# Attention and balanced expert layer on one core: token scaling moved into the attention, search steps split with ScalarE, operands rearranged

## The chip, the cores and the metric

The kernel runs on one core of a Trainium2 chip. The metric is the device time of one execution in microseconds (us), taken as the median of several runs. A ratio is the mean time of one kernel's fast runs over that of the other's fast runs of the same rounds, so it is not quite the ratio of the medians quoted beside it; its bracket is a 95% interval. All runs compared here are in the fast state, except two single looks (e7 and e10) whose state a single run cannot tell, and one run of the kernel before in the first batch, which counted as slow and is left out of the ratios.

In the profile, PE is TensorE (PEld its weight loads), DVE is VectorE, ACT is ScalarE, POOL is GpSimd. L266 is line 266 of the kernel that is being profiled.

## The reference

Attention without a softmax, then a layer of eight experts to which the tokens are dealt greedily, 576 to each:

```python
kv  = einsum('bhsd,bhse->bhde', k, v)            # B,H,S,D = 8,8,576,64
out = einsum('bhsd,bhde->bhse', q, kv)
x   = out / sqrt(mean(out**2) + 1e-6) * g_norm   # -> 4608 tokens x 512
logits = x @ w_gate                              # 8 experts
# go through all (token, expert) by falling logit; take it if the token
# is free and the expert has fewer than 576
for e in range(8):
    mask = assigned == e
    out[mask] = relu(x[mask] @ w1[e]) @ w2[e]    # 512 -> 1024 -> 512
```

## The kernel before

The kernel has three stages: the attention, which writes tokens to DRAM; a first search for the threshold that fills one expert; and the eight experts, in which TensorE multiplies for expert t while the other engines search the threshold and the token list of expert t+1.

A search step compares each token's best logit, `mx`, with 32 candidate thresholds. This is one VectorE instruction of 128 x 1152 elements, and TensorE then counts its result:

```python
def compare(over, cand, c0=0, c1=GC):                        # L266
    nc.vector.tensor_tensor(over[:, c0:c1],
        mx[:, c0:c1]...to_broadcast([P, c1 - c0, NCAND]),
        cand[:, 1:NCAND + 1]...to_broadcast([P, c1 - c0, NCAND]), op=AL.is_ge)

def candidates(s, lo, cand):
    nc.vector.tensor_scalar(cand, in0=away[:, s], scalar1=lo, scalar2=None, op0=AL.add)
...
sm = small_ps["step"][:, turn_of[0] % 2]                     # PSUM
ends, cand_ps = sm[:, 0:2], sm[:, 2:]
for g in range(G):                                           # four of them, VectorE
    nc.vector.tensor_scalar(ends[g * QP:(g + 1) * QP], in0=kk, scalar1=width[0:QP, s:s + 1],
                            scalar2=lo_was[0:QP], op0=AL.mult, op1=AL.add)
lo = ends[:, 1:2]
if s + 1 < NSTEP:
    compare(over, candidates(s + 1, lo, cand_ps))
```

The candidates from the second search on are in PSUM (`held_ps`). So the compare has **one input in SBUF and one in PSUM**.

The tokens come with an unscaled attention output and a factor, and VectorE scales them just before TensorE transposes them (five operations `xs` to an expert).

The search is a Python generator. Its `yield 4.6` says how much of TensorE's work (in us) is to be put in the program between two counts; the first layer's work comes in pieces of 0.487.

## Time and profile before

| | before |
|---|---|
| time, median of 3 runs | 712.15 us (708.46 to 715.15) |
| span of the profiled run | 709.6 us |
| first expert starts | 180.34 us |
| experts 0 to 7 together | 518.98 us |
| of that, TensorE busy | 509.62 us, so 9.4 us idle |

The two last rows are from a table of windows by expert, whose sum row is this (window lengths, then busy time of each engine):

```profile
sum 518.98, PE 509.62 PEld 397.33 DVE 333.63 ACT 89.80 POOL 244.81; mean PE 63.70 PEld 49.67 DVE 41.70 ACT 11.23 POOL 30.60
```

Two groups of the page, with busy time, mean ns of one, and the idle time before them and what ended most of it:

```profile
L266 DVE TENSOR_TENSOR over<-mx,held_ps 128x1152 bf16<-128x1152 f32 x42 | 56.9, 1354 | 1.5
L478 PE MATMUL n_ps<-best,over 128*128 128x32 bf16 x441 | 19.3, 179 | 21.1 <-DVE over L266 19.2
```

The 42 compares take 1354 ns each. Most of the 19.2 us that TensorE waits for them are waits of the first search, where nothing else runs (one of them is the 4.71 us in front of the first count).

### The profile page before, as it was taken

How to read it: one execution, taken by the hardware profiler on the slowest of the kernel's cores; microseconds unless marked ns; L12 is line 12 of the kernel's file. 1: busy time of each engine (PE TensorE's matmuls, PEld its weight loads, DVE VectorE, ACT ScalarE, POOL GpSimd, SP SyncE). 2: the span in 40 equal slices, each digit the busy share in tenths (PEclk: the TensorE clock that was granted, in tenths of full speed). 3: DMA queues.
4: the chain of work that ended last, by engine and by line, in shares of the span. 5: the costliest groups of instructions: out<-in, count | busy, mean ns of one | idle time of the engine just before them, and what ended most of it. 6: DMA issues, size and time to landing. Idle time of an engine off the chain costs nothing.

```text
span 709.6 us, 13280 instructions
## 1 busy us (share of the span) xinstructions
PE 616.8 (87%) x5370; PEld 482.7 (68%) x5370; DVE 443.3 (62%) x1393; ACT 155.9 (22%) x315; POOL 263.8 (37%) x249
## 2 busy tenths in 40 slices
PE   3787788214999899989998999999899999999994
PEld 2566666212778677857885788678677867877782
DVE  4344656888687778888878779887887545020011
ACT  1454555300211121022102111121112022112100
POOL 0100011002342562438344632735263659226322
PEclk9988977555999999999999999999999999999998
DMA  8987889405303600531081053108013843001001
GB/s 283 316 278 237 278 297 351 177 0 184 129 1 103 251 26 1 205 137 38 6 306 67 1 180 132 68 1 312 28 41 127 293 165 106 0 30 38 0 1 67
DMA packets 41405, 93.41 MB, mean 132 GB/s; under 512 B 3456, under 2 KB 3456, under 8 KB 41344
## 3 DMA queue, kind: packets, MB, share of 16 engines
q1 hardware_dynamic: 34752, 72.49, 29.1%
q0 software_dynamic: 5888, 20.06, 8.1%
q8 instruction: 42, 0.69, 0.4%
q14 instruction: 19, 0.16, 0.1%
q10 hardware_dynamic: 704, 0.02, 0.1%
HBM read 72.50 MB, written 20.05 MB: 130 GB/s over the span
## 4 chain that ended last, share of the span: by engine, by line
PE 74%; DVE 13%; issue 6%; DMA 4%; ACT 1%; POOL 1%; POOLq 0%; ACTq 0%; DVEq 0%
PE h_ps L798 35%; PE y_ps L847 20%; PE o_ps L370 3%; PE qt_ps L301 3%; PE y_ps L858 3%; PE kv_ps L313 3%; PE t_ps L747 2%; DVE over L266 2%; DMA xg<-x_dram,ids 2%; PE n_ps L478 2%; DVE xs L733 1%; DMA gw<-in_moe_w_gate_dram 1%; PE warm_ps L625 1%; DVE need L484 1%; DVE held_ps L524 1%
## 5 line engine op out<-in xcount | busy, mean ns | idle before, releaser
L798 PE MATMUL h_ps<-xt,w_sb 128*128 128x288 f32 x1024 | 260.1, 410 | 0.8 <-ACT xt L750 0.8
L798 PEld LDWEIGHTS h_ps<-xt,w_sb 128*128 128x128 f32 x1024 | 190.6, 190 | 55.4 <-issue 5.7
L801 ACT ACTIVATE hid<-h_ps 128x288 f32<-128x288 f32 x128 | 52.6, 411 | 208.1 <-PE h_ps L798 208.1
L847 PE MATMUL y_ps<-tw,sh 128*128 128x256 f32 x384 | 86.5, 380 | 0.0
L847 PEld LDWEIGHTS y_ps<-tw,sh 128*128 128x128 f32 x384 | 72.0, 190 | 9.3
L789 POOL TENSOR_TENSOR sh<-hid 128x512 f32<-128x512 f32 x32 | 41.7, 1303 | 94.4 <-ACT hid L801 94.3
L673 POOL DMA_INDIRECT xg<-x_dram,ids x40 | 38.6, 964 | 82.8 <-DVE ids L668 35.8
L750 ACT ACTIVATE xt<-t_ps,g_col 128x512 f32<-128x512 f32 (+1 forms) x40 | 25.8, 645 | 161.6 <-PE t_ps L747 161.6
L847 PE MATMUL y_ps<-w_sb,hid 128*128 128x256 f32 x256 | 57.8, 381 | 0.0
L266 DVE TENSOR_TENSOR over<-mx,held_ps 128x1152 bf16<-128x1152 f32 x42 | 56.9, 1354 | 1.5
L818 DVE TENSOR_TENSOR y_sb<-y_ps,u 128x512 f32<-128x512 f32 x24 | 16.4, 684 | 63.8 <-PE y_ps L847 63.8
L756 POOL DMA_INDIRECT out_dram<-y_sb,outs x32 | 33.4, 1043 | 52.1 <-issue 36.7
L847 PEld LDWEIGHTS y_ps<-w_sb,hid 128*128 128x128 f32 x256 | 48.1, 190 | 6.6
L524 DVE TENSOR_SCALAR held_ps<-held_ps,width 32x2 f32<-32x2 f32 x144 | 41.3, 287 | 5.3
L779 POOL TENSOR_TENSOR tw<-w_sb 128x512 f32<-128x512 f32 x32 | 39.9, 1269 | 12.4 <-DMA w_sb<-in_moe_w_dram 12.3
L478 PEld LDWEIGHTS <-over 128*128 128x128 bf16 x441 | 17.5, 97 | 38.8 <-DVE over L266 27.5
L370 PE MATMUL o_ps<-kvx,qt 64*64 64x72 f32 x1152 | 32.9, 261 | 9.8 <-issue 9.2
L733 DVE TENSOR_TENSOR xs<-xg 128x512 f32<-128x512 f32 (+1 forms) x40 | 31.9, 809 | 14.7 <-DMA xg<-x_dram,ids 8.1
L478 PE MATMUL n_ps<-best,over 128*128 128x32 bf16 x441 | 19.3, 179 | 21.1 <-DVE over L266 19.2
L370 PEld LDWEIGHTS o_ps<-kvx,qt 64*64 64x64 f32 x1152 | 26.8, 160 | 15.5 <-issue 14.1
L378 DVE TENSOR_REDUCE ms<-sq 128x8 f32<-128x512 f32 x36 | 24.1, 681 | 20.1 <-ACT sq L376 19.9
L327 POOL COPY kvx<-kv 64x512 f32<-64x512 f32 x16 | 9.8, 609 | 71.3 <-DVE kv L321 70.9
(203 smaller groups left out, 831.9 us busy)
## 6 DMA issues: line engine op xcount, KB each, us to landing
w_sb<-in_moe_w_dram SPq DMA_DIRECT2D x16, 1024.0 KB, 6.3
w_sb<-in_moe_w_dram SPq DMA_DIRECT2D x8, 2048.0 KB, 13.3
k_sb<-in_k_dram SPq DMA_DIRECT2D x16, 576.0 KB, 5.4
v_sb<-in_v_dram SPq DMA_DIRECT2D x16, 576.0 KB, 5.8
q_sb<-in_q_dram SPq DMA_DIRECT2D x16, 576.0 KB, 5.6
x_dram<-o_sb SPq DMA_DIRECT2D x16, 576.0 KB, 4.3
x_dram<-o_sb SPq DMA_DIRECT2D x4, 288.0 KB, 4.2
xg<-x_dram,ids POOLq DMA_INDIRECT x40, 5.4
```

Source lines behind the costliest of these rows:

```text
L266: nc.vector.tensor_tensor(over[:, c0:c1], mx[:, c0:c1].rearrange("p (c o) -> p c o", o=1).to_broadcast([P, c1 - c0, NCAND]), cand[:, 1:NCA ...
L370: nc.tensor.matmul(o_ps[n * HP:(n + 1) * HP, rp, (2 * r2 + l) * W:(2 * r2 + l + 1) * W], lhsT=turned_q[bn][ks, block // 2, l * HP:(l + 1) ...
L478: nc.tensor.matmul(n_ps, lhsT=over[:, c:c + G].rearrange("p c n -> p (c n)"), rhs=best[:, :, c:c + G], start=(c == 0), stop=(c == GC - G))
L524: nc.vector.tensor_scalar(ends[g * QP:(g + 1) * QP], in0=kk, scalar1=width[0:QP, s:s + 1], scalar2=lo_was[0:QP], op0=AL.mult, op1=AL.add)
L673: tokens = nc.gpsimd.indirect_dma_start(out=xg[0:nr].rearrange("p h w -> p (h w)"), out_offset=None, in_=x_dram, in_offset=bass.IndirectOf ...
L733: nc.vector.tensor_tensor(xs[0:nr].rearrange("p (h d) -> p h d", h=H), xg[0:nr, :, 0:D], xg[0:nr, :, D:D + 1].to_broadcast([nr, H, D]), op ...
L756: put = nc.gpsimd.indirect_dma_start(out=out, out_offset=bass.IndirectOffsetOnAxis(ap=ids_of[t][0:nr, n:n + 1], axis=0), in_=y_sb[0:nr, :] ...
L779: in_order(nc.gpsimd.tensor_tensor(o[:, m:m + 2], x[:, m:m + 2], y[:, m:m + 2], op=AL.subtract))
L789: in_order(nc.gpsimd.tensor_tensor(o[:, ms], x[:, ms], y[:, ms], op=op))
L798: nc.tensor.matmul(h_ps, lhsT=w1[:, 2 * (d % 2) + d // 2, f * P:(f + 1) * P], rhs=xt[:, d, cs], start=(d == 0), stop=(d == DC - 1))
L801: nc.scalar.activation(hid[:, f, cs], h_ps, ACT.Relu)
L847: nc.tensor.matmul(p_ps[:, n], lhsT=left[:, f, n * P:(n + 1) * P], rhs=right[:, f], start=(f == 0), stop=(f == FH - 1))
```

## The change

Its intent: take the scaling, and the wait it makes, out of the experts; take work off VectorE by giving a step's ends and candidates to ScalarE; put search operands into PSUM, so that VectorE and GpSimd collide less (the trace of before shows one such collision: 1.34 us instead of 0.46); and order the first layer by halves of the tokens, so that fewer token blocks are needed before it can begin. The core of the diff:

```diff
-        nc.gpsimd.tensor_copy(o_sb[:, :, :, D:D + 1]..., inv)
+        for t in range(T):                     # in the attention
+            if c0 + T <= last_own:
+                nc.gpsimd.tensor_tensor(xo[:, t], o_sb[:, t, :, 0:D], inv[...].to_broadcast([P, H, D]), op=AL.mult)
+            else:
+                for h in range(H):
+                    late.append(lambda t=t, h=h: nc.scalar.mul(xo[:, t, h], o_sb[:, t, h, 0:D], inv[...]))
...
-    for nm, shape in (("step", (2, NCAND + 3)), ("cut", (2, GC)), ("mx", (GC,)), ...
+    for nm, shape in (("hi", (2,)), ("cut", (2, GC)), ("mx", (GC,)), ..., ("half", (NB,)), ("rise", (2, GC))):
...
+    KNOWN = 1.6
+    def candidates(s, lo):
+        cand = small("cand_a", NCAND + 1)                      # a tile in SBUF
+        nc.scalar.activation(cand, row_f[:, 0:NCAND + 1], ACT.Identity, scale=width[:, s:s + 1], bias=lo)
+        return cand
...
-            yield 4.6 if s > 0 else 0.4 if first else 2.0 if t == 1 else 4.0
+            yield (4.6 if t == 0 else 4.8 - KNOWN) if s > 0 else 0.4 if first else 2.0 if t == 1 else 2.4
...
+                yield KNOWN
-                lo_was, (ends, cand_ps) = lo, pieces()
+                lo_was, ends = lo, small("ends", 2)
                 for g in range(G):
-                    nc.vector.tensor_scalar(ends[g * QP:(g + 1) * QP], in0=kk, ...)
+                    nc.scalar.activation(ends[g * QP:(g + 1) * QP], kk, ACT.Identity, scale=..., bias=...)
-                    compare(over, candidates(s + 1, lo, cand_ps))
+                    compare(over, candidates(s + 1, lo))
...
-            nc.vector.tensor_tensor(xs[0:nr]..., xg[0:nr, :, 0:D], xg[0:nr, :, D:D + 1].to_broadcast(...), op=AL.mult)
...
-        for f, c in [(f, c) for f in units for c in range(2)] if t else [(f, c) for c in range(2) for f in units]:
+        for c, f in [(c, f) for c in range(2) for f in units]:
```

## The prediction

> **What bounds the kernel now.** I read the page first, then a table of windows by stage, then the chain of waits, then TensorE's own timeline. The page's busy lines say which engine fills the span, and its list of waits says who holds it up.
>
> ```profile
> span 709.6 us, 13280 instructions
> ...
> PE 616.8 (87%) x5370; PEld 482.7 (68%) x5370; DVE 443.3 (62%) x1393; ACT 155.9 (22%) x315; POOL 263.8 (37%) x249
> ...
> PE 74%; DVE 13%; issue 6%; DMA 4%; ACT 1%; POOL 1%; POOLq 0%; ACTq 0%; DVEq 0%
> ```
>
> TensorE (PE) carries 74% of the chain that ended last. The stages differ, so I cut the span at the starts of the eight experts (columns: window, length, busy time and instructions of each engine, granted clock, DMA share, GB/s):
>
> ```profile
> 30.00:137.00 107.00, 78.17 (x2208) 64.91 (x2200) 61.29 (x145) 55.96 (x110) 10.72 (x23) 0.79 0.81 282
> 137.00:180.30 43.30, 13.74 (x105) 7.73 (x105) 35.99 (x144) 2.06 (x3) 4.93 (x5) 0.56 0.26 85
> 180.30:250.35 70.05, 67.69 (x367) 52.12 (x367) 52.01 (x173) 12.12 (x25) 30.30 (x26) 0.98 0.35 124
> 250.35:316.94 66.59, 64.25 (x352) 50.09 (x351) 55.20 (x176) 11.55 (x24) 29.66 (x25) 1.00 0.27 94
> 316.94:382.50 65.56, 63.73 (x359) 50.37 (x359) 52.18 (x176) 11.55 (x24) 32.39 (x28) 1.00 0.28 103
> 450.00:514.70 64.70, 62.21 (x343) 48.52 (x343) 53.77 (x174) 10.98 (x23) 31.23 (x28) 1.00 0.29 104
> 514.70:578.70 64.00, 64.00 (x330) 49.61 (x326) 41.20 (x128) 11.56 (x24) 32.71 (x28) 1.00 0.40 145
> 578.70:640.30 61.60, 61.60 (x284) 48.49 (x284) 18.86 (x30) 11.56 (x24) 31.61 (x27) 1.00 0.23 75
> ```
>
> Three stages: attention to 137 us; a serial first search (VectorE busy 36 of 43 us) to 180 us; experts from 180 to 699 us. Expert 6 shows an expert with no search: 61.6 us, TensorE without a gap. The others take 63 to 70. TensorE's timeline shows what fills the difference:
>
> ```profile
> 239.31 0.66 PE L747 MATMUL t_ps<-ident,xs 128*128 128x128 f32 x4 [2.32 <-DVE xs L733]
> 305.85 0.66 PE L747 MATMUL t_ps<-ident,xs 128*128 128x128 f32 x4 [2.35 <-DVE xs L733]
> 377.39 0.63 PE L747 MATMUL t_ps<-ident,xs 128*128 128x128 f32 x4 [1.83 <-DVE xs L733]
> 509.51 0.63 PE L747 MATMUL t_ps<-ident,xs 128*128 128x128 f32 x4 [1.86 <-DVE xs L733]
> ```
>
> The bracket is TensorE's idle time and its releaser: the transposes of the next expert's tokens wait for VectorE to scale them. That is what the change takes away.
>
> How much is there? Per expert TensorE needs 128 first-layer records at 0.244 us (31.24 us for 128 in the chain), 112 second-layer ones at 0.216, 16 of the rest block at 0.234, about 2.1 us of transposes, and 0.23 us for each of 7 search counts. I laid this out in program order, with the kernel's own pacing numbers, and compared the experts' measured starts (180.34, 250.35, 316.94, 383.25, 448.01, 515.53, 578.61). The excess over uninterrupted work is 5.5, 3.1, 2.6, 1.3, 3.8 and 0.3 us for experts 0 to 5: 16.6 us, of which some 9.4 are visible idle gaps. This is the ceiling of what any repair of these waits can return.
>
> [...]
>
> ```profile
> 221.49 0.46 DVE L563 SCALAR_TENSOR_TENSOR here<-two,here 128x288 f32<-128x288 bf16 x1
> 287.32 1.34 DVE L563 SCALAR_TENSOR_TENSOR here<-two,here 128x288 f32<-128x288 bf16 x1
> 286.63 1.72 POOL L789 TENSOR_TENSOR sh<-hid 128x512 f32<-128x512 f32 x1
> ```
>
> The same operation takes 0.46 us alone and 1.34 beside GpSimd, whose own took 1.72 instead of 1.27.[...]
>
> **The change, part by part.**
>
> Token scaling. Five VectorE operations of 0.68 us or more leave each expert, 31.9 us in all. Their time is off the path; what counts is the wait in front of the transposes. At the first expert the gather of block 0 has landed by 174.40 and its scaling takes 0.69, so transposes and everything after start about 0.7 us sooner; a little more if the gather starts nearer its indices (170.38 now, indices written at about 169.3). I take -0.9.
>
> The scaling moves to GpSimd in attention: 31 tiles at about 1.27 us (the duration of its 128x512 two-input operations) = 39 us spread over 100 us in which GpSimd is busy about a tenth. Five tiles go to ScalarE as 40 operations[...], in the first search, where ScalarE is idle and the tokens are not needed until 170. Free. But GpSimd's share is not: after the fourth and sixth batch VectorE runs the early choice (84.67 to 87.43 and 111.95 to 113.99), with some five operations that have two SBUF inputs[...] some 0.9 us: up to 4.5 us each time. In the trace VectorE is continuously busy there and feeds TensorE. About half should be hidden by gaps TensorE has at just those points (2.78 us before 89.86, 2.15 before 116.47): +2 each time, +1 in the last batch, -1 for 11% less written. I take +3.5, the term I trust least.
>
> Fewer buffers in flight let three writes instead of one go before the last loads: 2 extra, about 1 MB at 280 GB/s = 3.4 us later. The last load is issued at 99.90 and lands near 105; its second half is used at 117.5. Hidden.
>
> Ends and candidates on ScalarE. A search step loses 4 x 0.287 + 0.259 = 1.41 us of VectorE and gains five pointer-bias activations[...], plus two crossings: no shorter. Counts to next counts is still about 5 us of latency. But the step is split into 1.6 and 3.2 of nominal TensorE time, and each part is rounded up to whole pieces of 0.487: 4 + 7 = 11 instead of 10. So a step takes 5.65 us where it took 5.16, +3 us in six steps, and the last step's pause adds 2 before the assignment. Shorter pauses after it give some back. In the program's order the tokens' list for expert 1 comes 4.3 us later than before (in the sixth of seven products instead of the fifth), for expert 2 about 0, for later experts early enough.
>
> Search operands in PSUM remove the 0.9 us collisions: VectorE only, off the path.
>
> First layer by halves. Only three of five blocks must be transposed before the next expert starts, the first of them some 1.3 us later. This makes room for the gather. For experts 2 to 4 the gap between list and first transpose is over 10 us, more than the 5.4 us (median) to landing plus 1.5 for indices: their waits vanish, 2.6 + 1.3 + 3.8 = -7.7, less 0.7 for small remainders: -7. For expert 1's tokens: list 4 to 5 us later, landing about 7 us after issue (231.41 to 238.39 now), first transpose about 1 us later: the wait grows to 5 or 6 us: +1.5. For expert 2's tokens: same place within 1 us: 0.
>
> ScalarE runs in order: a search step waiting for VectorE's count, or one beside a 0.69 us eviction, delays a Relu. Between Relus it idles 1.53 us and has two PSUM buffers, so mostly hidden: +1.
>
> Sum: -0.9 + 3.5 - 7 + 1.5 + 0 + 1 = -1.9 us. From the 709.6 of the profile and the median of 712.15, 710. Because the pauses look tuned on a chip, and my position counting may be pessimistic for expert 1, I lean 2 us lower: 708.
>
> **Rivals.** A: all token waits vanish and attention costs nothing: -16.6 - 1 - 1 = about 693. For it: VectorE falls from 80% to some 60% in the experts. Against it: the gather's own landing stands behind the scaling in experts 0 and 1. B: GpSimd collisions are not hidden and the late list costs more: attention +9, expert 0 +4, ScalarE stalls +3, against -8: about 720.[...] Against it: the split that sends the last five tiles to ScalarE shows the author knew of it. C: the pieces cancel completely, 712.
>
> **Range and chances.** Runs of the same kernel spread from 708.46 to 715.15. With the attention term uncertain by 4 and the expert term by 6, the range is 699 to 718. Over 2% faster means under 697.9, nearly the ceiling of A: 0.09. Slower than 726.4 needs more than B: 0.03.
>
> **What would show it.** No scaling before transposes; idle before the transposes of experts 1 and 2's tokens released by the gather DMA, about 5 and 2 us; none for later ones. Search counts 5.6 us apart. The first search starts later than 137 by 2 to 5 us, with early-choice operations around 1 us; if it stays at 137 the attention term is wrong. Relu gaps longer than 1.53 followed by TensorE idle would show ScalarE in the way. Wrong if expert 0 no longer waits, or if the time falls under 699.

## More of the kernel before

At the start of each expert, GpSimd makes weight differences `tw` for the second layer, eight instructions of 128 x 512 in a row:

```python
for o, x, y in ((t1, b12, b11), (t2, b22, t1), (t3, b22, b12), (t4, t2, b21)):
    for m in range(0, FH, 2):
        in_order(nc.gpsimd.tensor_tensor(o[:, m:m + 2], x[:, m:m + 2], y[:, m:m + 2], op=AL.subtract))
```

The name `"mx"` in the PSUM list is a working copy that both kernels have; the `mx` that the compare reads is another tile, in SBUF in both.

## The result, and the profile after

The changed kernel takes **765.86 us** (764.18 to 766.57, four runs), the kernel before 712.02 in the same rounds: ratio 1.0754 [1.0701, 1.0808]. It is 7.5% slower, and the prediction (708, range 699 to 718) was wrong. The page's lines that answer to those in the prediction:

```profile
span 762.4 us, 13333 instructions
...
PE 633.4 (83%) x5370; PEld 489.3 (64%) x5370; DVE 397.6 (52%) x1158; ACT 241.2 (32%) x560; POOL 298.1 (39%) x271
...
PE 66%; DVE 19%; issue 6%; ACT 5%; DMA 3%; POOL 1%; POOLq 0%; ACTq 0%; DVEq 0%
```

VectorE did get less to do (397.6 us busy instead of 443.3), yet its share of the chain that ended last grew from 13% to 19%. So somewhere it has become the one that TensorE waits for. The windows by expert (columns as in the prediction) say where:

```profile
332.73:407.79 75.06, 66.43 (x361) 50.97 (x360) 50.06 (x134) 25.99 (x64) 32.10 (x27) 0.95 0.24 88
407.79:483.51 75.72, 67.13 (x358) 51.29 (x353) 50.18 (x138) 26.12 (x63) 32.84 (x29) 0.93 0.25 91
630.38:692.38 62.00, 62.00 (x285) 48.49 (x284) 9.05 (x25) 11.54 (x24) 30.69 (x27) 1.00 0.22 73
sum 570.91, PE 525.17 PEld 403.26 DVE 284.90 ACT 165.04 POOL 248.76; mean PE 65.65 PEld 50.41 DVE 35.61 ACT 20.63 POOL 31.10
```

The experts with a search take some 75 us instead of 65 to 67; expert 6 (from 630.38), which has none, takes 62.0 as before. The eight together grew by 570.91 - 518.98 = 51.9 us, nearly the whole of the 52.8 us by which the span grew; the first expert starts only 1.2 us later (181.56). TensorE's idle time in them went from 9.4 to 570.91 - 525.17 = 45.7 us, which is +36.4, and its busy time by +15.5 us for the same work. The granted clock (third column from the end: the share of full speed that TensorE's throttle let through) is 0.93 to 0.96 in experts 0 to 5, where it was 1.00 (0.98 in expert 0).

The groups of the page name the cause of the idle time:

```profile
L266 DVE TENSOR_TENSOR over<-mx,cand_a 128x1152 bf16<-128x1152 f32 x36 | 91.9, 2554 | 78.1 <-ACT cand_a L488 75.3
L508 PE MATMUL given_ps<-best,over 128*128 128x32 bf16 x441 | 19.6, 180 | 56.5 <-DVE over L266 54.8
L555 ACT ACTIVATE ends<-kk,ends,width 32x2 f32<-32x2 f32 x144 | 55.4, 385 | 33.5 <-DVE kk L550 30.3
```

The compare of the same size takes 2554 ns in the mean where it took 1354, and TensorE's wait for it has grown from 19.2 to 54.8 us, by 35.6, nearly all of the 36.4 us of new idle time. The row shows what is different: it reads `mx` and `cand_a`, both in SBUF. TensorE's timeline shows the waits one by one (start, length, instructions, and in brackets the idle time and its releaser):

```profile
246.74 1.12 PE L790 MATMUL t_ps<-ident,xg 128*128 128x128 f32 x4 [6.33 <-DMA xg<-x_dram,ids]
272.22 0.42 PE L508 MATMUL given_ps<-best,over 128*128 128x32 bf16 x9 [5.68 <-DVE over L266]
322.70 0.66 PE L790 MATMUL t_ps<-ident,xg 128*128 128x128 f32 x4 [2.58 <-DMA xg<-x_dram,ids]
346.43 0.42 PE L508 MATMUL given_ps<-best,over 128*128 128x32 bf16 x9 [8.63 <-DVE over L266]
346.69 4.93 PE L839 MATMUL h_ps<-xt,w_sb 128*128 128x288 f32 x14
```

Two more such waits are 8.59 us (before 422.40) and 6.38 us (before 497.22), and one of 5.95 lies before 572.3: one count wait in each of experts 1 to 5, 35.2 us together. The wait of 6.33 us is that for expert 1's tokens. What VectorE and GpSimd did in front of the count at 272.22:

```profile
263.77 8.39 DVE L266 TENSOR_TENSOR over<-mx,cand_a 128x1152 bf16<-128x1152 f32 x1 [2.13 <-ACT cand_a L488]
...
260.21 0.91 POOL L797 DMA_INDIRECT out_dram<-y_rest,outs  x1 [5.23 <-DVE y_rest L907]
261.13 2.51 POOL L820 TENSOR_TENSOR tw<-w_sb 128x512 f32<-128x512 f32 x2
263.58 2.50 POOL L820 TENSOR_TENSOR tw<-w_sb,tw 128x512 f32<-128x512 f32 x2
266.03 2.48 POOL L820 TENSOR_TENSOR tw<-w_sb 128x512 f32<-128x512 f32 x2
268.47 2.47 POOL L820 TENSOR_TENSOR tw<-tw,w_sb 128x512 f32<-128x512 f32 x2
```

The compare was released at 263.77, just after the third instruction of GpSimd's run of eight had begun at 263.58. It ended at 272.16: GpSimd's run ends at 268.47 + 2.47 = 270.94, and 1.2 us later, about the compare's own length, it is done. It was kept out by **all six instructions that were left**, the running one included, and not by that one alone. ScalarE then stood too (8.90 us before its next Relu), since it waited for TensorE.

### The profile page after: what moved, and what is told of

Its sections match the earlier page's. It is cut to its first block, busy times and chain, and to the rows that moved or that the text cites. A ratio compares the mean times of both kernels' runs of the same rounds, so it can differ in the third digit from the quotient of the medians.

```text
span 762.4 us, 13333 instructions
## 1 busy us (share of the span) xinstructions
PE 633.4 (83%) x5370; PEld 489.3 (64%) x5370; DVE 397.6 (52%) x1158; ACT 241.2 (32%) x560; POOL 298.1 (39%) x271
## 4 chain that ended last, share of the span: by engine, by line
PE 66%; DVE 19%; issue 6%; ACT 5%; DMA 3%; POOL 1%; POOLq 0%; ACTq 0%; DVEq 0%
PE h_ps L839 27%; PE y_ps L888 21%; DVE over L266 8%; PE y_ps L899 3%; PE qt_ps L301 3%; PE o_ps L372 3%; PE t_ps L790 2%; PE kv_ps L313 2%; ACT ends L555 2%; PE given_ps L508 2%; DMA xg<-x_dram,ids 2%; DMA gw<-in_moe_w_gate_dram 1%; DVE ms L380 1%; DVE need L514 1%; PE warm_ps L662 1%
## 5 line engine op out<-in xcount | busy, mean ns | idle before, releaser
L839 PE MATMUL h_ps<-xt,w_sb 128*128 128x288 f32 x1024 | 274.2, 423 | 0.8 <-ACT xt L793 0.8
L839 PEld LDWEIGHTS h_ps<-xt,w_sb 128*128 128x128 f32 x1024 | 195.9, 196 | 58.5 <-issue 4.1
L266 DVE TENSOR_TENSOR over<-mx,cand_a 128x1152 bf16<-128x1152 f32 x36 | 91.9, 2554 | 78.1 <-ACT cand_a L488 75.3
L830 POOL TENSOR_TENSOR sh<-hid 128x512 f32<-128x512 f32 x32 | 43.9, 1372 | 157.7 <-ACT hid L842 157.7
L714 POOL DMA_INDIRECT xg<-x_dram,ids x40 | 41.8, 1044 | 76.6 <-DVE held_ps L630 42.7
L508 PE MATMUL given_ps<-best,over 128*128 128x32 bf16 x441 | 19.6, 180 | 56.5 <-DVE over L266 54.8
L555 ACT ACTIVATE ends<-kk,ends,width 32x2 f32<-32x2 f32 x144 | 55.4, 385 | 33.5 <-DVE kk L550 30.3
L797 POOL DMA_INDIRECT out_dram<-y_sb,outs x32 | 31.4, 981 | 42.2 <-issue 28.6
L399 POOL TENSOR_TENSOR xo<-o_sb,inv 128x512 f32<-128x512 f32 x31 | 32.5, 1079 | 33.9 <-ACT sq L378 21.6
L820 POOL TENSOR_TENSOR tw<-w_sb 128x512 f32<-128x512 f32 x32 | 39.9, 1268 | 12.2 <-DMA w_sb<-in_moe_w_dram 12.0
L313 PE MATMUL kv_ps<-v_sb,k_sb 64*64 64x64 f32 x1152 | 28.2, 243 | 9.1 <-issue 9.1
L301 PE MATMUL qt_ps<-ident,q_sb 128*128 128x128 f32 x144 | 31.5, 348 | 4.3 <-ACT kvt L334 1.9
```

Of the source, the lines that this page charges most:

```text
L266: nc.vector.tensor_tensor(over[:, c0:c1], mx[:, c0:c1].rearrange("p (c o) -> p c o", o=1).to_broadcast([P, c1 - c0, NCAND]), cand[:, 1:NCA ...
L301: nc.tensor.transpose(t_ps[:, x, :], q_sb[:, (4 * n + x) * P:(4 * n + x + 1) * P], ident)
L313: nc.tensor.matmul(kv_ps[cs, l, r * D:(r + 1) * D], lhsT=k_sb[ls, r, j, :], rhs=v_sb[ls, r, j, :], start=(j < 2), stop=(j >= R - 2))
L508: nc.tensor.matmul(n_ps, lhsT=over[:, c:c + G].rearrange("p c n -> p (c n)"), rhs=best[:, :, c:c + G], start=(c == 0), stop=(c == GC - G))
L555: nc.scalar.activation(ends[g * QP:(g + 1) * QP], kk, ACT.Identity, scale=width[0:QP, s:s + 1], bias=lo_was[0:QP])
L714: tokens = nc.gpsimd.indirect_dma_start(out=xg[0:nr], out_offset=None, in_=x_dram, in_offset=bass.IndirectOffsetOnAxis(ap=ids[0:nr, n:n + ...
```

## The experiments

Ten kernels ran, all with correct results (the record has no e6 and no e9). A theory T and rivals were set against each other:

- **T**: the compare lost its PSUM input (the candidates went from PSUM to an SBUF tile, since ScalarE makes them) and, with both inputs in SBUF, is kept out by GpSimd's run (8.39 us instead of 1.36 at 263.77).
- **R1**: the two crossings to ScalarE, and ScalarE's work in the step, are what delays the counts.
- **R2**: the attention's scaling, or the halves of the first layer, cost it.

### e1: the changed kernel, with the compare's other operand in PSUM

The candidates stay where the change has them; a second copy of `mx` goes to PSUM, and the compare reads that.

```diff
+    now = {"mx": mx}
             nc.vector.tensor_tensor(mx, m, gone, op=AL.add)
+            now["mx"] = small_ps["mx_all"]
+            nc.vector.tensor_tensor(now["mx"], m, gone, op=AL.add)
-            over[:, c0:c1], mx[:, c0:c1]...
+            over[:, c0:c1], now["mx"][:, c0:c1]...
-                      ("rise", (2, GC))):
+                      ("rise", (2, GC)), ("mx_all", (GC,))):
```

> The changed kernel with one extra 36-element VectorE operation per search that keeps a second copy of the tokens' best values in PSUM; the compare of searches 1 to 6 reads that copy, so it has one SBUF input (the candidates of ScalarE) instead of two. Theory T (the compare lost 8 to 11 us in each of five experts because both its inputs are now in SBUF[...]): every compare returns to 1.36 us, no wait of TensorE for it over 1 us in the experts, time about 718 us (765.9 less 38 of waits and 10 of stretched first-layer matmuls). Rival S (ScalarE in order: ends and candidates there make the step longer and hold up Relus): stays above 750 us. Rival H (halves of the first layer): stays above 750 us.

Measured: **716.29 us** (715.01 to 719.66), ratio to the kernel before 1.005 [0.9983, 1.0116]. 50 us came back with one operand moved. The compare's row, the same compare in the same place, and the GpSimd pair that runs across it:

```profile
L269 DVE TENSOR_TENSOR over<-held_ps,cand_a 128x1152 bf16<-128x1152 f32 x36 | 48.9, 1357 | 73.4 <-ACT cand_a L491 70.6 <-ACT ends L558 2.8
...
265.09 1.36 DVE L269 TENSOR_TENSOR over<-held_ps,cand_a 128x1152 bf16<-128x1152 f32 x1 [2.13 <-ACT cand_a L491]
264.91 2.50 POOL L823 TENSOR_TENSOR tw<-w_sb,tw 128x512 f32<-128x512 f32 x2
```

1.36 us in the middle of GpSimd's run, where it had been 8.39, and neither engine slows the other. TensorE's waits for the counts in experts 1 to 5 are gone; what stays is one wait of 6.30 us for expert 1's tokens and one of 2.53 for expert 2's. R1 and R2 cannot be the bulk: ScalarE's part, the scaling and the halves are all still in.

### e2: the kernel before, with only the candidates moved to SBUF

The converse. VectorE still makes them (by another operation, a `tensor_tensor` instead of a `tensor_scalar`), so ScalarE has no part in it.

```diff
+    def in_sbuf(s, lo):
+        cand = small("cand_s", NCAND + 1)
+        nc.vector.tensor_tensor(cand, away[:, s], lo.to_broadcast([P, NCAND + 1]), op=AL.add)
+        return cand
-                    compare(over, candidates(s + 1, lo, cand_ps))
+                    compare(over, in_sbuf(s + 1, lo))
```

> The kernel before, whose only edit is that the candidates of a step from the second search on are written to SBUF instead of PSUM, still by VectorE. Theory T: in five of six searches a compare meets GpSimd's run of eight operations and lasts 8 to 11 us, so 30 to 45 us slower than before, about 745 to 757 us. Rivals S and H: no change, 712 us.

Measured: **761.0 us** (760.39 to 765.16), ratio 1.0697 [1.062, 1.0775]. That is somewhat more than expected, and it makes nearly all of the change's loss with none of the change's other parts.

```profile
L266 DVE TENSOR_TENSOR over<-mx,cand_s 128x1152 bf16<-128x1152 f32 x36 | 93.0, 2583 | 1.2
```

### e3: the changed kernel, with ends and candidates back on VectorE, in PSUM

```diff
-    def candidates(s, lo):
-        cand = small("cand_a", NCAND + 1)
-        nc.scalar.activation(cand, row_f[:, 0:NCAND + 1], ACT.Identity, scale=width[:, s:s + 1], bias=lo)
+    def candidates(s, lo, cand):
+        nc.vector.tensor_scalar(cand, in0=away[:, s], scalar1=lo, scalar2=None, op0=AL.add)
...
-                    nc.scalar.activation(ends[g * QP:(g + 1) * QP], kk, ACT.Identity, ...)
+                    nc.vector.tensor_scalar(ends[g * QP:(g + 1) * QP], in0=kk, ...)
```

> The changed kernel with ends and candidates back on VectorE and in PSUM; places of the search pieces, halves and token scaling stay as changed. Theory T: compares of 1.36 us, time 710 to 718 us, within 3 us of the run with the second copy in PSUM. Rival S: also near 712, but then the run with the copy in PSUM stays above 750. Rival H: above 750.

Measured: **714.2 us** (711.39 to 718.62), ratio 1.0013 [0.9943, 1.0083]. Beside e1 it says that, with the change's own pacing and every compare short again (1354 ns in the mean), it makes little who computes the ends: the medians differ by 2 us, the eight experts in the profiles by 1 (523.3 against 524.2), and the intervals overlap. Its expert 1 still waits 6.40 us for its tokens.

### e4: the kernel before, with only the scaling moved to the attention

> The kernel before with the token scaling alone moved into attention (GpSimd 31 tiles, ScalarE 5), everything else as before. Attention ends 2 to 3 us later, the first expert starts 1 us earlier after that, and the transposes wait for the gather alone: -1 for expert 1, up to -2 each for experts 2, 3 and 5. Sum about 707 us; 712 if the gather lands no sooner than VectorE was done; above 720 only if the scaling part is what made the changed kernel slow.

```diff
-        nc.gpsimd.tensor_copy(o_sb[...], inv)
+        ... xo = o_sb * inv on GpSimd, the last tiles on ScalarE, as in the change
-            nc.vector.tensor_tensor(xs[0:nr]..., xg..., op=AL.mult)
-            scaled.append(xs)
+            scaled.append(xg)
```

Measured: **701.72 us** (698.01 to 705.16), ratio 0.9838 [0.9758, 0.9918]. It beats both kernels, and by more than expected (the interval lies below 1, but on both sides of a gain of 2%). In its profile the waits before the transposes are 1.86 us (expert 1) and 0.71 us (expert 2), where they were 2.32 and 2.35, and none is over 0.3 us in the later ones.

### e5: e4, and the first layer by halves

```diff
-        for f, c in [(f, c) for f in units for c in range(2)] if t else [...]:
+        for c, f in [(c, f) for c in range(2) for f in units]:
```

(and the main loop's places for the transposes as in the change; the search's pauses stay those of before)

> The kernel with the scaling alone in attention (701.7 us) plus the first layer by halves and the later transposes of the change; places of the search pieces, VectorE's ends and candidates stay those of before. If the late list of the changed places is what the changed kernel still loses once its compare is mended (experts 0 and 1 took 73.8 and 69.7 us against 68.1 and 64.9): expert 0 about 67, expert 1 about 64.5, the waits of 1.86 and 0.71 us for the gather gone, 0.4 to 1 us more in each later expert, time 699 to 704 us. If the halves are what it loses: experts 0 and 1 above 70 and 67, time above 708.

Measured: **703.75 us** (699.8 to 706.07), ratio 0.990 [0.9862, 0.9938]. In the profiles, experts 0 and 1 take 66.3 and 64.4 us against 68.1 and 64.9 in e4, and each later one up to 1 us more: about nothing in sum. The halves did make room for the gather (one wait of 1.20 us is left in all), but in e4 there was little left to hide.

### e7 and e10: what keeps the compare out for a whole run?

Both keep two SBUF inputs. e7 makes GpSimd start its run of eight only after the fifth Relu, so that it no longer follows directly on the indirect DMA that GpSimd issues. e10 leaves it where it is and makes it 16 instructions of 256 elements.

```diff
-            for m in range(0, FH, 2):                                   # e10
-                in_order(nc.gpsimd.tensor_tensor(o[:, m:m + 2], ...))
+            for m in range(FH):
+                in_order(nc.gpsimd.tensor_tensor(o[:, m:m + 1], ...))

+            tc.add_manual_dep(made[0].ins, relu.ins.name, ...)          # e7: the run's first waits for a Relu
```

> The changed kernel with GpSimd's run of eight weight differences held until the fifth Relu of the first layer, so that GpSimd is idle for some us between its last indirect DMA issue and the run, as it was in expert 0, where a compare got in after one operation (2.2 us). If the run keeps VectorE out to its end only because it follows an indirect DMA issue directly: all compares under 2.7 us, time under 730. If the run's own operations keep it out: some compares still of 6 to 11 us in experts 1 to 5, time 750 to 770.

> The changed kernel with the run of eight GpSimd differences cut into sixteen of half the size, the same work. If a compare waits for one operation of the run: the long compares shrink from 8 to 11 us to under 3, time about 720. If it waits for the end of the run: they stay 8 to 12 us, as the run grows a little with its fixed costs, time 765 to 775.

Measured, one run each: e7 **720.94 us**, e10 **713.11 us**. In both no compare takes over 2.45 us (means 1502 and 1508 ns). A compare of e7 with the GpSimd pair that began during it, and one of e10 likewise:

```profile
278.25 1.63 DVE L266 TENSOR_TENSOR over<-mx,cand_a 128x1152 bf16<-128x1152 f32 x1 [2.38 <-ACT cand_a L488]
278.62 3.60 POOL L822 TENSOR_TENSOR tw<-tw,w_sb 128x512 f32<-128x512 f32 x2
```

```profile
258.61 1.45 DVE L266 TENSOR_TENSOR over<-mx,cand_a 128x1152 bf16<-128x1152 f32 x1 [2.13 <-ACT cand_a L488]
258.70 3.99 POOL L820 TENSOR_TENSOR tw<-w_sb,tw 128x256 f32<-128x256 f32 x4
```

Four instructions of 256 elements take 2.77 us together in e10 (at 262.66), two of 512 in the changed kernel 2.48 (at 266.03).

In e7 VectorE waits 0.27 us for the rest of the GpSimd instruction that ran when it came, and then GpSimd gives way: its next pair takes 3.60 us instead of 2.5. So in e7 the two take turns, one instruction at a time. In the changed kernel and in e2 they did not: all ten compares that met the run in experts 1 to 5 waited until its end (6.7 to 9.7 us over their 1.36; the longest took 11.05 us, in e2), at whatever point of an instruction they came, from just before its start to 1.15 us into it. In expert 0, where GpSimd had idled for 12 us before the run, they got in after one instruction in both kernels (2.20 and 1.71 us). So in these kernels the long exclusion took both, the run directly behind an indirect DMA's issue and instructions of 512 elements; each was taken away in one run. Both together are not always enough: at 537.55 in the changed kernel a compare met another run of 512-element instructions (`sh`) behind an indirect DMA, and got in after one (1.93 us). There GpSimd had stood for 0.08 us between the first two, while those of the long cases follow without a pause. **Why** a run keeps its hold, the profile does not show, and this stays open.

### e8: e4, with GpSimd's scaling held until after VectorE's early choice

```diff
+        made = compare(over0, cand0, c0, c1)          # the last operation of the early choice
+        for do in held_back:
+            tc.add_manual_dep(do().ins, made.ins.name, ...)
...
-                nc.gpsimd.tensor_tensor(xo[:, t], ...)
+                held_back.append(lambda t=t: nc.gpsimd.tensor_tensor(xo[:, t], ...))
```

> The kernel with the scaling alone in attention, with GpSimd's scalings of the fourth and sixth batch held until VectorE's early choice there is done. If the choice's two-input operations beside GpSimd are what made attention end 2.5 to 4 us later: the first expert's start 2 to 4 us earlier and about 699 us. If not, 701.7 as before; if GpSimd's copies of the next batch then come late, 703 to 706.

Measured: **698.73 us** (694.58 to 703.6), ratio 0.9826 [0.9783, 0.987], the lowest median of all that ran. The two early choices take VectorE 2.75 and 2.04 us, where e4's take 4.93 and 4.51, and the first count of the first search is at 135.51 us, where e4 has it at 140.94. The ratios do not tell e8 from e4, e5 or e12; the early choices do. A middle expert of it, with no gap and the clock at full:

```profile
374.20:438.20 64.00, 64.00 (x353) 50.14 (x351) 50.12 (x166) 11.56 (x24) 30.43 (x28) 1.00 0.30 106
```

### e11: e1, and the pauses of the kernel before

After e1, the eight experts still take 524.2 us where e5's take 510.1. What e5 lacks is ScalarE's part, the change's other pauses, and its rearranged small operands and deferred operations. Are these 14 us the late list of tokens?

```diff
-    KNOWN = 1.6
+    KNOWN = 1.4
-            yield (4.6 if t == 0 else 4.8 - KNOWN) if s > 0 ...
+            yield (4.6 if t == 0 else 4.6 - KNOWN) if s > 0 ...
-        yield 5.0 if t == 1 else 5.4
+        yield 5.4 if t == 0 else 3.6 if t == 1 else 4.0
```

> The changed kernel with a copy of mx in PSUM (as in e1) and, beside that, the old pacing of a search: 3 + 7 pieces of TensorE's work to a step instead of 4 + 7, and the pause that a search leaves behind taken off the pause before the assignment. Theory ([...]what is left of the loss against the better kernels is the late list of tokens): the steps come 5.2 us apart instead of 5.7, the list for expert 1 some 4 us sooner, the 6.3 us wait before expert 1's transposes falls to 1 to 3 us, the 2.5 us one of expert 2 to 0 to 1; time 706 to 710, ratio 0.990 to 0.997. Rival (ScalarE's place in a step makes it longer than 5.2 us, and its 2 crossings cannot be hidden in 10 pieces): TensorE waits at the counts, 0.3 to 1 us each, and the time stays at 713 to 718.

Measured: **710.75 us** (708.68 to 718.25), ratio 1.0003 [0.9947, 1.0059]: in between. The counts that make expert 1's list came at 232.81 us instead of 237.82 (1.7 of the 5.0 us are an earlier start of the first expert), and the 6.30 us wait for expert 1's tokens shrank to 0.2; the eight experts take 518.1 us instead of e1's 524.2. But the steps did not come 5.2 us apart. They stayed at 5.7 on average (counts at 190.52, 196.27, 202.19, 207.65). In part this is because TensorE now waits for a Relu that stands behind a step in ScalarE's order; two steps of this search have such a wait, of 0.49 us each:

```profile
200.63 1.72 PE L842 MATMUL h_ps<-xt,w_sb 128*128 128x288 f32 x6 [0.49 <-ACT hid L845]
```

So the rival was right about the steps and the theory about the list. Some 6 us of the 14 went with the late list. Some 8 us stay against e5's experts (518.1 against 510.1). 3.7 of them are visible as waits, for Relus, counts and sums (5.0 us idle in experts 0 to 5 instead of 1.25); the other 4 lie in time that counts as busy, and no run here takes them apart. The Relu waits belong to the ScalarE step; that the rest of the 8 us does too is not shown, since e5 lacks other edits as well and e3 with the old pauses did not run.

### e12: e8 and the halves together

The edits of e5 and e8 in one kernel.

> Both best parts together: scaling in the attention with GpSimd's share held until after VectorE's early choice (as in e8), and the first layer by halves with the old pauses (as in e5). If halves are worth what e5 and e4 showed (experts 0 and 1 some 2.3 us shorter together, the six later ones 0.3 us longer each on average), they cancel: 698 to 700, ratio 0.981 to 0.986. If e5's first two experts keep their gain and the later ones' loss was chance: 696, ratio 0.979.

Measured: **700.33 us** (697.44 to 705.29), ratio 0.9858 [0.9804, 0.9912]. As the first of the two expectations had it, the halves bring nothing on top of e8.

### The versions side by side

| kernel | compare's inputs | scaling | halves | ends made by | median us | ratio |
|---|---|---|---|---|---|---|
| before | SBUF, PSUM | in the experts | no | VectorE | 712.02 | 1 |
| after | SBUF, SBUF | attention | yes | ScalarE | 765.86 | 1.0754 |
| e2 | SBUF, SBUF | in the experts | no | VectorE | 761.0 | 1.0697 |
| e1 | PSUM, SBUF | attention | yes | ScalarE | 716.29 | 1.005 |
| e3 | SBUF, PSUM | attention | yes | VectorE | 714.2 | 1.0013 |
| e11 | PSUM, SBUF | attention | yes | ScalarE, old pauses | 710.75 | 1.0003 |
| e5 | SBUF, PSUM | attention | yes | VectorE, old pauses | 703.75 | 0.990 |
| e4 | SBUF, PSUM | attention | no | VectorE, old pauses | 701.72 | 0.9838 |
| e12 | SBUF, PSUM | attention, held | yes | VectorE, old pauses | 700.33 | 0.9858 |
| e8 | SBUF, PSUM | attention, held | no | VectorE, old pauses | 698.73 | 0.9826 |

The single runs of e7 and e10 are left out.

## Why the prediction was wrong

**The step that failed** is this one: "Search operands in PSUM remove the 0.9 us collisions: VectorE only, off the path." It took the change's title at its word. Smaller operands (`rise`, `half`, `hi`, `mid`) did go into PSUM, but the operands of the largest instruction of a search went the other way: `mx` stayed in SBUF, and the candidates left PSUM, because ScalarE now writes them into an SBUF tile. The diff shows it, in the line `cand = small("cand_a", NCAND + 1)`, and the prediction had shown a VectorE operation with both inputs in SBUF (`here`) that took 1.34 us beside GpSimd instead of 0.46. It did not ask whether the same could happen to the compare. Where an operand did go into PSUM, the step was right: the `up` instructions that read `rise` from there took 0.34 us at most, where one took 6.15 before. e1 (one operand moved, 50 us back) and e2 (one operand moved, 48 us lost) show that this alone makes the loss.

**Its size** would have been missed even so. If a meeting costs at most one GpSimd instruction, as the 0.9 us of `here` suggest, and there is about one meeting in each of five experts, an estimate from the 2.5 us per pair of such instructions gives up to 5 x 1.25 = 6 us for all. Measured were 39.9 us in five compares (7.03, 9.56, 9.38, 7.17 and 6.74 over the usual 1.36), because each was kept out to the end of the run. The kernel before already held one such case, and the prediction overlooked it. In its expert 6, `up`, with two SBUF inputs, came at 585.14, 3.9 us into the run of eight, and took 6.15 us where its shortest takes 0.33; it ended at 591.29, the run at 591.09. It is off the path there, and in the table of groups it shows only in the mean of 802 ns:

```profile
L688 DVE TENSOR_TENSOR up<-less,rise 128x180 f32<-128x180 f32 x16 | 12.2, 802 | 0.0
```

The prediction took the 0.9 us of one other collision as the size of all.

**A second cost** was nowhere in the prediction: TensorE's clock. The granted clock falls to 0.50 during each of the six waits of over 5 us and stays there for 6.8 or 10.2 us; after the wait of 8.63 us the 14 multiplications at 346.69 take 4.93 us, where the same 14 take 3.64 in e1. TensorE was busy for 28.6 us inside these six stretches; the kernel before has one, with 3.4 us. If all of this work went at half speed, it cost 14.3 - 1.7 = 12.6 us (an estimate), most of the 15.5 us that TensorE was busy longer. After shorter waits it did not always fall. In the kernel before it fell to 0.50, for 3.4 us, just after a wait of 2.32 us, and the multiplications slow down in the same way after 2.35 (e2: six `y_ps` take 2.57 us, six a little later 1.46), 2.53, 3.11 and 2.29 (e1, e3 and e7: eight take 3.40 to 3.47, eight a little later 1.89) and 2.28 (e10: five take 2.48, eight a little later 1.89), but not after 2.58 in the changed kernel or 2.35 in the kernel before's expert 1. What decides it there, these runs do not show. In e5, e8 and e11, where no wait is over 2 us, the granted clock is 1.00 in every expert that was measured (the first six in e5, all in e8 and e11).

The other steps, in the order of the prediction:

- **Attention, +3.5 us, "the term I trust least"**: right in cause, about right in size. The first count came at 139.44 instead of 136.90, +2.5. The operations of the early choice do take longer beside GpSimd's scaling, as these rows of the kernel after and the one before show:

```profile
84.92 1.17 DVE L247 TENSOR_SCALAR lg<-lg,bound,bottom 128x128 f32<-128x128 f32 x1
```

```profile
84.67 0.34 DVE L247 TENSOR_SCALAR lg<-lg,bound,bottom 128x128 f32<-128x128 f32 x1
```

  The two choices take 4.93 and 4.52 us instead of 2.76 and 2.04, together +4.7 us of VectorE's time, and in e8, with the scaling held back, 2.75 and 2.04 again: so it was avoidable. How much of it reaches the first count, single profiles cannot say: with the scaling not held back it comes at 134.8 (e10) to 141.7 us (e1) in eight kernels, at 134.0 and 136.9 without the scaling (e2, before), and at 134.9 and 135.5 with it held back (e12, e8).
- **The first expert sooner, -0.9**: right. From the first count to its start it is 42.1 us instead of 43.4, -1.3.
- **The waits for later experts' tokens, -7**: right in kind, too large in size. The waits are gone, in the changed kernel and in e4. Experts 2 to 4 together took 198.6 us before and take 193.1 in e4 and 195.0 in e1: -5.5 and -3.6.
- **Expert 1's tokens, whose list comes late: +1.5, by a wait of "5 or 6 us"**: the wait is 6.33 us. Its size is right; its cost was more. From 2.32 us before, a wait of 5 or 6 is already some 3 us more and not 1.5, and 6.33 is 4.0 more; besides, the clock fell (1.12 us for the four transposes, 0.60 at full speed), and e4 shows that the same wait was to be had at 1.86.
- **Expert 2's tokens, about 2 us as before**: 2.58 us.
- **Steps 5.65 us apart instead of 5.16, +3 in six**: right. In e1's first expert the six steps take 35.8 us (186.28 to 222.06) where they took 32.0 (182.87 to 214.82), +3.8; some are 5.65 apart (198.88, 204.53, 210.18), others 6.2 to 6.5.
- **Two more writes before the last loads, 3.4 us, hidden**: 1 MB at the 282 GB/s of the window from 30 to 137 us is rather 3.6 us (an estimate); no run tests it alone.
- **ScalarE in order, +1**: a Relu that waits for a step was indeed hidden by the change's pauses, and e11 shows that without them it is not (two waits of 0.49 us). The five activations of a step, each with two pointer operands, a scale and a bias, measure 385 and 416 ns, and the scaling with one pointer 332 ns.

The **rivals** A, B and C missed as well: none of them had a new wait at the compare. B named the kind of loss (collisions with GpSimd that are not hidden), but put it in the attention.

The reading of the profile of before, that the scaling's waits and their repair are worth a handful of us, was sound: e4 is that part alone, at -1.6%. The change spent it, and 50 us more, on one operand's place.

## What to carry to other kernels

Before moving who writes an operand, list for each large VectorE instruction where every input lies before and after, because an instruction whose input leaves PSUM can be kept out by GpSimd's work (here 8.10 to 10.92 us instead of 1.36), and a producer's change does that without touching the consumer's line. A wait on the path can cost TensorE its clock as well (here all six of over 5 us did, at 0.50 for 6.8 or 10.2 us), so price it above its length. Look at the longest instruction of a group and not only at its mean: one of 6.15 us was there to be seen before the change. And test the parts of a bundled change one by one: here one part was worth 1.6%, one nothing, and one cost 7%.
